# Pooled values of batch 0 summed in PSUM from the tokens' rows, wider filler matmuls, and new numbers for the planner

## The chip, the cores and the metric

The kernel runs on one NeuronCore of a Trainium2 chip. The metric is device time in microseconds (us) for one execution of the program. TensorE (PE), VectorE (DVE), ScalarE (ACT), GpSimd (POOL) and SyncE (SP) each take their instructions in a fixed order and wait for one another by semaphores; SP issues nearly all DMAs.

## The reference, cut to what matters

q, k, v are (4, 8, 576, 64), all float32. `x` has 2304 rows of 512.

```python
q_d, k_d, v_d = (t.reshape(B, H, 144, 4, D).mean(axis=3) for t in (q, k, v))
out_d = softmax(q_d @ k_d.T / 8) @ v_d                # pooled attention, 144 x 144
out_local = softmax(where(|i - j| < 4, q @ k.T / 8, -1e9)) @ v
x = (repeat(out_d, 4, axis=2) + out_local)            # to 2304 x 512
h = x @ moe_w_in;   x = elu(h) @ moe_w_out            # 512 -> 2048 -> 512
h = x @ moe2_w_in;  return (s * relu(h)**2 + b) @ moe2_w_out
```

## The kernel before, in words

**Feed-forward layers.** Every operand is split into a high part that TensorE multiplies at its fast float32 rate and a low part, the rest; a product is three passes (high x high, low x high, high x low). Phase 0 is the first layer, phase 1 the second. Tokens go in groups j of 256 (or 512 where "wide"), the 2048 hidden columns in 16 blocks f. `ffn_h` (matmuls at L894) makes the hidden block, ScalarE, VectorE and GpSimd apply the activation and split it, `ffn_x` (L960 to L967) multiplies it on into PSUM. The weights of phase 0 pass once through two staging buffers `raw`: two DMAs of 512 KB (L347, L351), then a chain on ScalarE (L356), VectorE (L359, L364), ScalarE (L303, the high part) and GpSimd or VectorE (L311, the low parts, 512 columns each) into `w0` to `w15`. In phase 0 the groups j = 0 and j = 1 run interleaved, j = 1 behind j = 0 by `LB` blocks, so that each weight block serves both while the others are still on their way.

**Attention.** Batches 0 and 1 work in units of two heads (`hp` = 0 to 3), batches 2 and 3 in another way. Batch 0 comes first of all, since nothing else can run without it; its data lie in the not yet used weight buffers: q and k in `w4` to `w7`, v in `w8` to `w11`, transposed q and k, pooled sums and the pooled v (`vd`) in `w12` to `w15`. `attention0` does the first half (288 tokens) of each unit, `attention0_rest` the second. The steps of a half: `tr` transposes (L535) and pools by a reduce (L541); `gs` makes pooled scores (L562) and their softmax; `ls` makes local scores (L647, L654) and their softmax; `gpt_` and `lpt_` transpose the probabilities (L610, L711); `gpv` multiplies the pooled ones by `vd` (L627); `lpv` multiplies the local ones by windows of v (L726), adds `up`, the result of `gpv`, and splits the sum into the operand x of phase 0.

**The pooled values.** `vg` holds, per partition, the four tokens of one pooled position side by side, for four head halves. `vsum` adds them in two tensor_tensor instructions (L548: 512 columns, in place; L549: 256 columns into `vd`), on GpSimd or VectorE. The late windows of v (`loads_late`, the second half's, L485) land where `vg` lay and so wait for `vsum`.

**The local softmax** has two forms: with `by_act` six ScalarE exponentials with row sums per half (L681); otherwise VectorE subtracts the maximum (L688, L689) and one ScalarE exponential does all (L693), and VectorE makes the sums. In batch 0, `by_act` holds for every unit.

**The order of the work** is written out by a planner (`Plan.emit`): every operation has a cost in us per engine, a due time, buffers and dependencies. It steps through a modelled time, picks per engine the operation that is ready and due first (with rules `HOLD`, `GROUP`, `WAIT`), and emits it. A DMA's length in the model is its bytes at 255 GB/s, times `slow`. Due times come from anchors (`T0`, `P0`, `TR`, `A1`, ...), pulled earlier by what depends on them. Where PE is idle in the model, `keep_warm` fills the time with matmuls on zeros (L1178, 128 columns each), so that its clock stays up.

**The end.** The last group's outputs leave through `ev` and `xr` buffers; the last two accumulators are copied in halves, by ScalarE and VectorE, and SP issues the DMAs (L989).

Of the kernel before, what the change touches and what calls it, by code (L numbers as in the profile page):

```python
# [22 lines left out]
EARLY = 1  # L23
ACT_EXP = 2
NLP = 2

T0, P0, LB, TR, R0, P1, P2 = 36.7, 5.112, 5, 34.78, 2.153, 2.551, 2.603
VO, N0, N1, WL, RL, A1, A2, A3, AE, XL = 1.82, -8.98, 62.49, 12.66, -44.23, 25.59, -36.48, 2.6, 63.87, 29.58  # L30
DE, DS, DT = -11.16, 96.84, 75.88
LASTP, NREST, VP = 2, 5, -9.3
# [22 lines left out]
class Plan:  # L55
# [5 lines left out]
    SLACK = 0.0  # L61
    GROUP = 18.61
    SWITCH = 0
    HOLD = 0.057
    WAIT = 1.615
# [162 lines left out]
def attn_moe_moe2(ctx, tc, q, k, v, w_in, w_out, w2_in, w2_out, s2, b2, mask, mask_d, out):  # L228
# [105 lines left out]
    def weights(ph, f):  # L334
# [9 lines left out]
        for i in range(2):  # L344
            def ld(i=i):
                if i == 0:
                    nc.sync.dma_start(  # L347
                        out=raw()[:, 0].rearrange("p (c f) w -> p c (f w)", c=CC),
                        in_=wi[:, f * 128:(f + 1) * 128].bitcast(I32).rearrange("(c p) f -> p c f", p=128))
                else:  # L350
                    nc.sync.dma_start(  # L351
                        out=raw()[:, 1].rearrange("p f w -> p (f w)"), in_=wo[f * 128:(f + 1) * 128, :].bitcast(I32))

            load(rawp[i], 524288, ld, due - RL, u=[raw])

# [41 lines left out]
    class Unit:  # L397
# [46 lines left out]
        def loads(self, due, late=0, nb=0.0, nb_late=0.0):  # L444
# [9 lines left out]
            def parts(i, n0, n1, late):  # L454
                for a in range(2):
                    e = "act" if a and not late and b == 0 and hp < 2 else "sp"
                    load(self.natp[i, n0 // NQB], 24576 * (n1 - n0),
                         lambda a=a, e=e: nat(i, n0, n1, a, nc.scalar if e == "act" else nc.sync),
                         due + (late if late else 0), u=[self.nat], slow=1.2, nb=nb + (nb_late if late else 0), queue=e)

# [11 lines left out]

            load(self.vg, 294912, vg, due + VO, u=self.both if b == 0 else (), nb=nb)

# [13 lines left out]
            def loads_v(half):  # L488
                for a in range(2):
                    load(self.vwp[half], VR * NQB * CT * 256, lambda a=a: vw(half, a),  # L490
                         due + VO + (late if half else 0), r=[self.vd] if b == 0 and half else (), u=self.both,
                         n=3 if (b, hp, a, half) == (0, 0, 0, 0) else 1, slow=1.2, nb=nb + (nb_late if half else 0))

# [51 lines left out]
        def vsum(self, due):  # L545
            def f(e):
# [4 lines left out]
            op(("pool", "dve"), (2.1, 1.3), (lambda: f(nc.gpsimd), lambda: f(nc.vector)),  # L551
               r=[self.vg], w=[self.vg, self.vd], u=self.both + self.tdv if self.b == 0 else (), due=due, lock=True)

# [65 lines left out]
        def gpv(self, halves, due):  # L619
            n = len(halves)  # L620
            ps = self.ps([128, n * G], "h" if halves[0] == 0 else "at")
            pt = [self.gpt[a, halves] for a in range(2)]

            def pe():
                for a in range(2):
                    for kc in range(2):
                        nc.tensor.matmul(ps()[a * D:(a + 1) * D, :], lhsT=self.vd()[:, 2 * a + kc, :],  # L627
                                         rhs=pt[a][0]()[:, pt[a][1], kc, :], start=(kc == 0), stop=(kc == 1))

            op("pe", 0.1 + 0.24 * n, pe, r=[self.vd, pt[0][0], pt[1][0]], w=[ps], u=self.tdv, due=due)  # L630
            if self.b >= DIRECT:
# [30 lines left out]
        def softmax(self, pss, half, due):  # L662
# [55 lines left out]
        def lpv(self, half, due):  # L718
# [19 lines left out]
            for j in range(2) if b == 0 else ():  # L738
                lo, hi = max(j * N, t0), min((j + 1) * N, t0 + HS)
                if hi > lo:  # L740
                    split(x_buf(0, j), hp, lo - j * N, hi - lo, lambda lo=lo, hi=hi: xf(lo - t0, hi - lo), [x], due)
            lo = max(t0, 2 * N) if b == 0 else t0
# [138 lines left out]
    def ffn_h(ph, j, f):  # L881
# [18 lines left out]
        if (ph, j) == (0, 0) and f < EARLY:  # L900
            runs = [([(0, 0, c), (1, 0, c), (0, 1, c)], [w_hi, w_lo, *x.part[c]]) for c in range(CC)]
        elif f == 0 or (ph, j) == (0, 0):
# [40 lines left out]
    def ffn_x(ph, j, f, g):  # L943
# [8 lines left out]
        for k, a in enumerate((2, 3, 0, 1) if two and last else range(tiles)):  # L952
# [19 lines left out]
            final = ph == 1 and j == NSUB - 2  # L972
            o = Buf(p2, "xr" if final and k < 2 else "ev", [128, 512])
            if ph == 0:
# [7 lines left out]
                continue  # L982
            parts = 2 if final and k >= 2 else 1
            n = 512 // parts
            for i in range(parts):
                half, c = Buf(None, "half", None), slice(i * n, (i + 1) * n)
                copy(lambda o=o, c=c: o()[:, c], lambda acc=acc, c=c: acc()[:, c], n, ("act", "dve")[i:] if parts > 1 else ("act", "dve"),
                     r=[acc], w=[half], u=[o], due=due - 4)
                load(Buf(None, "out", None), 262144 // parts, lambda a=a, o=o, c=c: nc.sync.dma_start(  # L989
                    out=out[j * N + a * 128:j * N + (a + 1) * 128, c], in_=o()[:, c]), due, r=[half], u=[o])  # L990

# [45 lines left out]
    def attention0():  # L1037
# [28 lines left out]
    def attention0_rest():  # L1066
        second = (1,)

        def A(u, d):
            u.tr(1, 1, d)  # L1070

# [102 lines left out]
    def keep_warm(slot, us, cold):  # L1174
        pool, tag = slot
        o = pool.tile([128, 128], F32, tag=tag, name=tag)
# [66 lines left out]
```

## Time and profile before

| | us |
|---|---|
| time, median of 3 runs (lowest, highest) | 951.03 (948.11, 952.88) |
| profiled execution, its own time | 953.3 |
| its span, first to last instruction | 951.5 |
| PE busy | 939.4 (99%) |
| DVE, ACT, POOL busy | 522.2, 438.9, 414.0 |
| mean granted TensorE clock | 0.995 |

The page's second part divides the span into 40 slices of 23.8 us; a digit is the busy share in tenths. Matmuls are pipelined, their ends are modelled, and fillers count as busy, so a 9 for PE doesn't say that it did useful work.

```profile
PE   8899999999999999999999999999999999999998
DVE  5466768887998969887245864222222322222221
ACT  6587775555544555444656664222322232223222
POOL 4477566798887786875556744000200110000000
PEclk9799999999999999999999999999999999999999
DMA  9739676543434543333244461000200010001001
```

### The profile page before, as it was taken

To read this page: it belongs to the slowest core of one execution; us is meant where nothing else is said; L and a number is where in the kernel's file an instruction comes from. 1 tells how busy PE (TensorE), PEld (TensorE's weight loads), DVE (VectorE), ACT (ScalarE), POOL (GpSimd) and SP (SyncE) were. 2 spreads that over 40 slices of the span, in tenths; PEclk is the share of its full clock that TensorE was granted. 3 is DMA by queue.
4 is the path that set the end of the run, shared out by engine and by line. 5 is a ranking of instruction groups with operands and counts; after the bars stand their busy time and mean duration, and the time that the engine had idled before them with its cause. 6 is when DMAs were issued, how large, how long until landed. Compare 5 with 4: busy or idle time off the path is not lost.

```text
span 951.5 us, 18034 instructions
## 1 busy us (share of the span) xinstructions
PE 939.4 (99%) x7096; PEld 826.2 (87%) x7096; DVE 522.2 (55%) x868; ACT 438.9 (46%) x1068; POOL 414.0 (44%) x378
## 2 busy tenths in 40 slices
PE   8899999999999999999999999999999999999998
PEld 7888999999999999999888898888888888888886
DVE  5466768887998969887245864222222322222221
ACT  6587775555544555444656664222322232223222
POOL 4477566798887786875556744000200110000000
PEclk9799999999999999999999999999999999999999
DMA  9739676543434543333244461000200010001001
GB/s 193 213 106 218 194 197 156 141 132 100 121 93 107 125 114 100 75 105 117 82 162 147 159 226 45 23 1 0 67 23 1 13 54 1 1 1 45 0 1 45
DMA packets 101941, 88.14 MB, mean 93 GB/s; under 512 B 48864, under 2 KB 90848, under 8 KB 101856
## 3 DMA queue, kind: packets, MB, share of 16 engines
q1 hardware_dynamic: 100064, 86.54, 32.4%
q8 instruction: 56, 0.92, 0.4%
q10 hardware_dynamic: 1792, 0.44, 0.2%
q14 instruction: 29, 0.24, 0.1%
HBM read 73.85 MB, written 13.11 MB: 91 GB/s over the span
## 4 chain that ended last, share of the span: by engine, by line
PE 88%; DVE 4%; ACT 2%; issue 2%; DMA 2%; POOL 2%; SPq 0%; DVEq 0%; POOLq 0%; ACTq 0%
PE h L894 37%; PE acc L964 14%; PE acc L967 12%; PE at L967 9%; PE acc L894 2%; PE at L960 2%; PE acc L960 2%; PE at L726 1%; PE at L1178 1%; DMA nat<-in_q_dram 1%; DVE raw L834 1%; DMA vg<-in_v_dram 1%; PE acc L1178 1%; PE at L627 1%; PE h L726 1%
## 5 line engine op out<-in xcount | busy, mean ns | idle before, releaser
L894 PE MATMUL h<-x,w 128*128 128x256 f32 (+1 forms) x1936 | 342.4, 323 | 1.4 <-DVE r L927 0.6
L894 PEld LDWEIGHTS h<-x,w 128*128 128x128 f32 x1936 | 285.1, 189 | 34.5 <-DVE r L927 1.3
L964 PE MATMUL acc<-gh,w 128*128 128x256 f32 x896 | 147.7, 286 | 0.0
L964 PEld LDWEIGHTS acc<-gh,w 128*128 128x128 f32 x896 | 122.3, 189 | 2.6 <-issue 1.9
L933 DVE SCALAR_TENSOR_TENSOR wu<-wu,sb,h 128x512 f32<-128x512 f32 x64 | 47.8, 747 | 128.5 <-ACT wu L932 128.5
L311 POOL TENSOR_TENSOR gl<-r,gh 128x256 fp32r<-128x256 f32 x98 | 88.9, 911 | 44.7 <-ACT gh L303 40.5
L932 ACT ACTIVATE wu<-h 128x512 f32<-128x512 f32 x64 | 38.3, 598 | 127.2 <-PE h L894 126.8
L311 POOL TENSOR_TENSOR w<-raw,w 128x512 fp32r<-128x512 f32 x50 | 68.7, 1390 | 50.3 <-ACT w L303 49.6
L964 PE MATMUL acc<-gl,w 128*128 128x256 f32 x448 | 89.9, 282 | 0.0
L964 PEld LDWEIGHTS acc<-gl,w 128*128 128x128 f32 x448 | 68.8, 188 | 0.0
L303 ACT ACTIVATE gh<-r 128x256 fp32r<-128x256 f32 x109 | 44.4, 413 | 44.1 <-PE acc L964 22.3
L834 DVE TENSOR_REDUCE raw<-wu 128x128 f32<-128x896 f32 x36 | 63.5, 1791 | 1.6 <-POOL wu L311 1.6
L311 POOL TENSOR_TENSOR wu<-raw 128x896 f32<-128x896 f32 x28 | 59.8, 2147 | 9.1 <-DVE raw L834 7.8
L923 ACT ACTIVATE r<-h 128x256 f32<-128x256 f32 x92 | 34.8, 378 | 59.8 <-PE h L894 32.1
L927 DVE SCALAR_TENSOR_TENSOR r<-r,h 128x256 f32<-128x256 f32 x92 | 37.6, 414 | 33.5 <-ACT r L925 31.4
L311 POOL TENSOR_TENSOR nat<-xr,x 128x256 fp32r<-128x256 f32 (+1 forms) x16 | 17.1, 1085 | 86.5 <-PE h L894 77.9
L894 PE MATMUL h<-nat,w 128*128 128x512 f32 x192 | 52.4, 394 | 0.0
L364 DVE SCALAR_TENSOR_TENSOR raw<-raw 128x1024 int32<-128x1024 int32 x32 | 46.7, 1460 | 9.3 <-ACT raw L356 8.0
L311 POOL TENSOR_TENSOR raw<-xr,x 128x256 fp32r<-128x256 f32 x16 | 12.1, 783 | 88.5 <-DVE x L305 80.6
L925 ACT ACTIVATE r<-r 128x256 f32<-128x256 f32 x112 | 46.7, 417 | 2.8
L894 PEld LDWEIGHTS h<-nat,w 128*128 128x128 f32 x192 | 36.0, 188 | 8.5
L303 ACT ACTIVATE w<-raw 128x1024 fp32r<-128x1024 f32 x32 | 36.4, 1138 | 10.7 <-DVE raw L364 10.4
(188 smaller groups left out, 1649.1 us busy)
## 6 DMA issues: line engine op xcount, KB each, us to landing
raw<-in_moe_w_in_dram SPq DMA_DIRECT2D x32, 512.0 KB
raw<-in_moe_w_out_dram SPq DMA_DIRECT2D x32, 512.0 KB
raw<-in_k_dram SPq DMA_DIRECT2D x17, 320.0 KB
raw<-in_v_dram SPq DMA_DIRECT2D x17, 320.0 KB
x2d<-ev SPq DMA_DIRECT2D x18, 256.0 KB
xr<-x2d SPq DMA_DIRECT2D x18, 256.0 KB
out_dram<-ev SPq DMA_DIRECT2D x14, 256.0 KB
vg<-in_v_dram SPq DMA_DIRECT2D x12, 288.0 KB
```

Of the source, the lines that this page charges most:

```text
L303: a = (0.11 + n / 1200, lambda: nc.scalar.activation(out=out(), in_=src(), func=ACTF.Copy, scale=scale))
L311: f = lambda e: lambda: e.tensor_tensor(out=out(), in0=in0(), in1=in1(), op=alu)
L364: nc.vector.scalar_tensor_tensor(out=low(), in0=high(), scalar=3, in1=low(), op0=ALU.logical_shift_left, op1=ALU.bitwise_or)
L834: op("dve", 0.07 + 14 * D / 546, lambda: nc.vector.tensor_reduce(out=vo()[:, WD + j * D:WD + (j + 2) * D].rearrange("p (j d) -> p j d", j= ...
L894: nc.tensor.matmul(ps(), lhsT=w()[:, wpart, 0, c * 128:(c + 1) * 128], rhs=x.at(xpart)[:, c, :], start=first and i == 0, stop=last and i = ...
L925: op("act", ta, lambda: nc.scalar.activation(out=e(), in_=e(), func=ACTF.Exp, scale=-1.0), r=[r1], w=[r2], u=[e], due=due)
L927: op("dve", td, lambda: nc.vector.scalar_tensor_tensor(out=e(), in0=e(), scalar=-1.0, in1=ps(), op0=ALU.add, op1=ALU.max), r=[r2, ps], w=[ ...
L932: op("act", ta, lambda: nc.scalar.activation(out=e(), in_=ps(), func=ACTF.Relu), r=[ps], w=[r1], u=[e], due=due)
L933: op("dve", td + 0.07, lambda: nc.vector.scalar_tensor_tensor(out=e(), in0=e(), scalar=sb2[:, 0:1], in1=ps(), op0=ALU.mult, op1=ALU.mult), ...
L960: nc.tensor.matmul(acc(), lhsT=wo[:, a * 128:(a + 1) * 128], rhs=g(), start=first, stop=end)
L964: nc.tensor.matmul(acc()[:, c * N:(c + 1) * N], lhsT=wo[:, cc * 128:(cc + 1) * 128], rhs=g(), start=first and c == 0, stop=end and c == 1)
L967: nc.tensor.matmul(acc(), lhsT=g()[:, a * 128:(a + 1) * 128], rhs=wo, start=first, stop=end)
```

## The change

- `gpv` for the first halves of batch 0 multiplies the probabilities by the four rows of `vg` directly: 8 matmuls per head that add up in PSUM, not 2 on `vd`; the two heads alternate. It no longer needs `vsum`, and is costed 1.3 us.
- `vsum` of batch 0 moves from `attention0` to `attention0_rest`, and waits for that `gpv` (`g1`), as it writes `vg` in place; the late windows of v follow it.
- The local softmax of unit hp = 3 of batch 0 leaves the `by_act` form (`ACT_EXP`, and `hp % 2` becomes `hp`).
- Fillers are 512 columns wide (the zero tile read four times by a broadcast), with 128-column ones for the rest.
- DMA lengths in the planner's model: weights 0.72 (1.0 before), `vg` 0.8 (1.0), q, k and windows of v 1.38 (1.2). `HOLD` goes to 0, `GROUP` to 18.85.
- Anchors: `T0` 38.32, `P0` 4.508, `LB` 4, `TR` 24.02, `P1` 2.468, `VO` 2.88, `RL` -33.19, `DE`, `DS`, `DT` slightly; the pieces of x of a first half that belong to group j = 1 are due 10 us later (`X1`).
- The first `ffn_h` has its last contraction block in two runs, the low part of x alone in the second.
- At the end the halves have buffers of their own, VectorE copies the first and ScalarE the second, whose DMA ScalarE issues.

```diff
-ACT_EXP = 2
+ACT_EXP = 3
-T0, P0, LB, TR, R0, P1, P2 = 36.7, 5.112, 5, 34.78, 2.153, 2.551, 2.603
+T0, P0, LB, TR, R0, P1, P2 = 38.32, 4.508, 4, 24.02, 2.153, 2.468, 2.603
+X1 = 10.0
-    HOLD = 0.057
+    HOLD = 0
...
-               r=[self.vg], w=[self.vg, self.vd], ...
+               r=[self.vg] + ([self.g1] if self.b == 0 else []), w=[self.vg, self.vd], ...
...
+            raw = self.b == 0 and halves[0] == 0
+            parts = [(kc, r) for kc in range(2) for r in range(4 if raw else 1)]
             def pe():
-                for a in range(2):
-                    for kc in range(2):
-                        nc.tensor.matmul(ps()[a * D:(a + 1) * D, :], lhsT=self.vd()[:, 2 * a + kc, :],
-                                         rhs=pt[a][0]()[:, pt[a][1], kc, :], start=(kc == 0), stop=(kc == 1))
+                for kc, r in parts:
+                    for a in range(2):
+                        w = self.vg()[:, 2 * a + kc, r * D:(r + 1) * D] if raw else self.vd()[:, 2 * a + kc, :]
+                        nc.tensor.matmul(ps()[a * D:(a + 1) * D, :], lhsT=w, rhs=pt[a][0]()[:, pt[a][1], kc, :],
+                                         start=(kc, r) == parts[0], stop=(kc, r) == parts[-1])
-            by_act = self.b == 0 and self.hp % 2 < ACT_EXP
+            by_act = self.b == 0 and self.hp < ACT_EXP
...
-            u.gs((0, 1), first, d), u.ls(0, d), u.vsum(d + VP)
-            u.loads_late()
+            u.gs((0, 1), first, d), u.ls(0, d)
...
-            u.tr(1, 1, d)
+            u.vsum(d + VP), u.loads_late(), u.tr(1, 1, d)
...
-        for _ in range(int(us / (128 / (1200.0 if cold else 2400.0) + 0.003))):
-            nc.tensor.matmul(o, lhsT=wz, rhs=wz, start=True, stop=True)
+        for n in (512, 128):
+            one = n / (1200.0 if cold else 2400.0) + 0.004
+            for _ in range(int(us / one)):
+                nc.tensor.matmul(o[:, :n], lhsT=wz, rhs=wz[:, None, :].to_broadcast([128, n // 128, 128]), start=True, stop=True)
+                us -= one
```

## Rows read from the trace of the kernel before

**Rows 1.** Busy time by stage: us, each engine's busy (instructions), clock, DMA, GB/s

```profile
0.00:38.00 38.00, 32.61 (x582) 28.67 (x583) 19.73 (x58) 24.60 (x104) 18.69 (x37) 0.94 0.95 199
38.00:90.00 52.00, 50.97 (x724) 46.37 (x725) 29.86 (x71) 38.37 (x132) 33.39 (x33) 0.95 0.64 170
90.00:300.00 210.00, 208.40 (x2262) 198.65 (x2262) 171.87 (x309) 120.15 (x336) 160.23 (x144) 1.00 0.52 140
```

**Rows 2.** The same stages, line L1178 alone: PE, PEld busy

```profile
0.00:38.00 38.00, 13.34 (x167) 12.08 (x167) 0.94 0.95 199
38.00:90.00 52.00, 11.15 (x139) 8.58 (x139) 0.95 0.64 170
```

**Rows 3.** Chain of work that ended last, 0 to 60 us: start, us, what

```profile
18.51 0.41 PE h L627 x8
...
19.15 0.46 PE acc L654 x34
19.61 1.17 PE h L726 x36
20.78 0.65 PE at L535 x6
...
28.49 2.36 issue
...
32.47 1.52 PE h L726 x36
33.99 0.68 PE h L627 x8
34.68 1.16 PE at L535 x6
35.83 2.06 PE h L726 x36
37.90 1.58 PE h L894 x6
...
49.93 0.80 PE at L1178 x14
```

**Rows 4.** DMA queues, 28 to 31 us: kind, packets, MB, share

```profile
q8 instruction: 1, 0.02, 2.8%
```

**Rows 5.** Busy time by stage, 33.2 to 43.5 us (columns as in Rows 1)

```profile
33.20:43.50 10.30, 10.30 (x102) 9.52 (x99) 4.70 (x7) 5.23 (x12) 5.87 (x6) 0.50 0.56 152
```

**Rows 6.** Line L681 by stage: ACT busy (instructions), clock, DMA, GB/s

```profile
22.00:28.00 6.00, 1.72 (x12) 1.00 1.06 342
```

**Rows 7.** Lines L688, L689, L693: durations min/median/max in ns

```profile
L688 DVE TENSOR_REDUCE lmx<-at x16: 253/265/276, 91.3 to 185.9; 96x3 f32<-96x114 f32 x16
L689 DVE TENSOR_TENSOR p<-at,lmx x16: 272/273/274, 91.6 to 186.2; 96x114 f32<-96x114 f32 x16
L693 ACT ACTIVATE p<-p x8: 382/396/416, 92.4 to 186.5; 96x228 f32<-96x228 f32 x8
```

**Rows 8.** POOL in order of time: start, us, line, idle before and its end

```profile
22.00 1.26 POOL L548 TENSOR_TENSOR w<-w 72x512 f32<-72x512 f32 x1 [0.23 <-DMA w<-in_v_dram]
23.35 0.82 POOL L549 TENSOR_TENSOR w<-w 72x256 f32<-72x256 f32 x1
...
34.05 1.30 POOL L311 TENSOR_TENSOR w<-raw,w 128x512 fp32r<-128x512 f32 x1 [4.73 <-ACT w L303]
```

**Rows 9.** SP in order of time: start, us, line

```profile
32.26 3.13 SPq L485 DMA_DIRECT2D w<-in_v_dram  x4
...
39.16 0.38 SPq L347 DMA_DIRECT2D raw<-in_moe_w_in_dram  x1
```

**Rows 10.** ACT in order of time: start, us, line

```profile
46.97 1.14 ACT L356 ACTIVATE raw<-raw 128x1024 f32<-128x1024 f32 x1
```

**Rows 11.** Chain of work that ended last, 938 to 952 us

```profile
947.46 0.39 ACT ev L303
...
947.88 0.42 DVE ev L305
```

More of the change, by code (lines that the diff above doesn't have):

```diff
@@ L61 @@
     SLACK = 0.0
-    GROUP = 18.61
+    GROUP = 18.85
     SWITCH = 0
-    HOLD = 0.057
+    HOLD = 0
     WAIT = 1.615
@@ L352, in ld @@
                         out=raw()[:, 1].rearrange("p f w -> p (f w)"), in_=wo[f * 128:(f + 1) * 128, :].bitcast(I32))
-            load(rawp[i], 524288, ld, due - RL, u=[raw])
+            load(rawp[i], 524288, ld, due - RL, u=[raw], slow=0.72)
         op("act", 0.11 + 2 * DM / 1200, lambda: nc.scalar.activation(
@@ L458, in parts @@
                          lambda a=a, e=e: nat(i, n0, n1, a, nc.scalar if e == "act" else nc.sync),
-                         due + (late if late else 0), u=[self.nat], slow=1.2, nb=nb + (nb_late if late else 0), queue=e)
+                         due + (late if late else 0), u=[self.nat], slow=1.38, nb=nb + (nb_late if late else 0), queue=e)
             parts(0, 0, 2 * NQB, 0)
@@ L471, in vg @@
                     in_=v[b, 2 * hp:2 * hp + 2].rearrange("a (h i r) d -> i (a h) (r d)", h=2, r=4))
-            load(self.vg, 294912, vg, due + VO, u=self.both if b == 0 else (), nb=nb)
+            load(self.vg, 294912, vg, due + VO, u=self.both if b == 0 else (), nb=nb, slow=0.8)
             def vw(half, a):
@@ L491, in loads_v @@
                          due + VO + (late if half else 0), r=[self.vd] if b == 0 and half else (), u=self.both,
-                         n=3 if (b, hp, a, half) == (0, 0, 0, 0) else 1, slow=1.2, nb=nb + (nb_late if half else 0))
+                         n=3 if (b, hp, a, half) == (0, 0, 0, 0) else 1, slow=1.38, nb=nb + (nb_late if half else 0))
             loads_v(0)
@@ L551, in vsum @@
             op(("pool", "dve"), (2.1, 1.3), (lambda: f(nc.gpsimd), lambda: f(nc.vector)),
-               r=[self.vg], w=[self.vg, self.vd], u=self.both + self.tdv if self.b == 0 else (), due=due, lock=True)
+               r=[self.vg] + ([self.g1] if self.b == 0 else []), w=[self.vg, self.vd], u=self.both + self.tdv if self.b == 0 else (), due=due, lock=True)
         def gs(self, heads, halves, due):
@@ L740, in lpv @@
                 if hi > lo:
-                    split(x_buf(0, j), hp, lo - j * N, hi - lo, lambda lo=lo, hi=hi: xf(lo - t0, hi - lo), [x], due)
+                    split(x_buf(0, j), hp, lo - j * N, hi - lo, lambda lo=lo, hi=hi: xf(lo - t0, hi - lo), [x], due + (X1 if j > half else 0))
             lo = max(t0, 2 * N) if b == 0 else t0
@@ L900, in ffn_h @@
         if (ph, j) == (0, 0) and f < EARLY:
-            runs = [([(0, 0, c), (1, 0, c), (0, 1, c)], [w_hi, w_lo, *x.part[c]]) for c in range(CC)]
+            runs = [([(0, 0, c), (1, 0, c), (0, 1, c)], [w_hi, w_lo, *x.part[c]]) for c in range(CC - 1)]
+            runs += [([(0, 0, CC - 1), (1, 0, CC - 1)], [w_hi, w_lo, x_hi[-1]]), ([(0, 1, CC - 1)], [w_hi, x_lo[-1]])]
         elif f == 0 or (ph, j) == (0, 0):
@@ L972, in ffn_x @@
             final = ph == 1 and j == NSUB - 2
-            o = Buf(p2, "xr" if final and k < 2 else "ev", [128, 512])
+            parts = 2 if final and k >= 2 else 1
+            os = [Buf(p2, "xr" if final and (k < 2 or i) else "ev", [128, 512]) for i in range(parts)]
+            o = os[0]
             if ph == 0:
@@ L982, in ffn_x @@
                 continue
-            parts = 2 if final and k >= 2 else 1
             n = 512 // parts
[L985 to L990, printed above, removed]
+            for i, o in enumerate(os):
+                c = slice(i * n, (i + 1) * n)
+                copy(lambda o=o, n=n: o()[:, :n], lambda acc=acc, c=c: acc()[:, c], n, ("act", "dve")[1 - i:][:1] if parts > 1 else ("act", "dve"),
+                     r=[acc], w=[o], due=due - 4)
+                e = "act" if parts > 1 and i else "sp"
+                load(Buf(None, "out", None), 262144 // parts, lambda a=a, o=o, c=c, n=n, e=e: (nc.scalar if e == "act" else nc.sync).dma_start(
+                    out=out[j * N + a * 128:j * N + (a + 1) * 128, c], in_=o()[:, :n]), due, r=[o], queue=e)
     def load_x(ph, j):
```

10 lines of the change are left out of this document (6 added, 4 removed).

## The prediction

> **What bounds the kernel now.** I read the page's busy shares first, then the stages, then the chain of waits and the queues of the first 90 us. PE is busy 99% of the span, so at first sight only less matmul work could help. The stages say otherwise. From 90 us on PE is busy 208.4 of 210 us [rows 1], and nearly all of that is real work: that part moves as a block. The first 90 us are not so full: 167 of the 582 matmuls before 38 us, and 139 of 724 up to 90 us, are fillers [rows 1, 2]. A stretch of 14 fillers takes 0.80 us in the chain [rows 3], 57 ns each; that makes 167 x 57 ns = 9.5 us and 139 x 57 ns = 7.9 us in which PE had nothing to do. Before 38 us other engines and the DMA queues (share 0.95) make the operand x; between 38 and 90 us PE waits for weight blocks and for the second halves. So the end is set by how soon the first 90 us come to full work, and what they save the rest keeps.
>
> Two losses stand out in the chain. At 28.49 PE stands still for 2.36 us for nothing that the profile shows ("issue"), in the middle of a stretch of fillers, where no semaphore can hold it [rows 3]. In those 3 us one 16 KB packet of PE's instruction queue was moved (q8), with the DMA queues full [rows 4]: I read it as PE running out of instructions. After it the clock falls: 0.50 from 33.2 to 43.5 us, the lower of its two levels, 1.2 GHz [rows 5].
>
> **The change part by part.** The sum is made against the profiled execution: span 951.5 us, own time 953.3 us. The median of the runs is 951.03, 2.27 less; I take that off at the end.
>
> *The instruction wait and the clock.* A wide filler does the work of four narrow ones, so 167 become 42 or somewhat more, say 65: about 100 matmuls, each with its weight load, leave PE's instruction stream before 38 us. The pooled sums put back 24 per unit (below), 72 for three units before the wait: the stream up to 28 us is a little shorter, and filler time no longer uses it up at one matmul per 57 ns. The late windows of v, two DMAs for each of four units, the last of them issued at 32.3 to 35.4 us now [rows 9], move behind vsum and leave the crowded queue. Both ends are open: the wait may stay (0) or go (-2.36). I take -2.36, the nearer since filler speed is what emptied the buffer. If PE doesn't stand still, the clock has no reason to fall there; what it cost before the first ffn_h is read from the same instructions at both levels: L726 1.52 and 2.06 against 1.17, L627 0.68 against 0.41, L535 1.16 against 0.65 [rows 3], together 0.35 + 0.89 + 0.27 + 0.51 = 2.02 us. Ends 0 and -2.02; I take -2.02. The lower clock after 38 us I cost at nothing: fillers lie between the ffn_h there and would take the room. A wide filler itself isn't in the trace; it fills planned idle time, so at four times 57 ns it costs 0, and an overrun by one filler, 0.23 us, in each of some ten stretches bounds it at +2.3. What gives way: 0.
>
> On the first of these the Trainium skill (Runtime: NRT & Kernel Launch, Instruction fetch mechanics) says that instructions are refilled in blocks of 16 KiB, 256 instructions, and that crossing a block is mostly hidden. The block's size is the q8 packet's; the hiding is not what the 2.36 us show. By that rule a shorter instruction stream brings nothing, and the sum is 4.4 us smaller; that is case C below.
>
> *The pooled sums on PE.* gpv of a first half now takes 8 matmul instructions in 0.41 us, 51 ns each [rows 3]; four rows instead of one make it 32, 1.64 us, +1.23. Its rate among alternating heads isn't shown: the nearest rows are L654's 34 in 0.46 us, 14 ns each, which would make 32 of them 0.43 (+0.02), and L627 at the lower clock, 0.68/8 = 85 ns, 2.72 (+2.3). I take 51 ns, the same instruction. For units 0 to 2 it lies in filler time (9.5 us before 38 us, of which it takes 3.7; were that cover gone it would cost those 3.7); for unit 3 it is in the chain between the transposed probabilities and the first ffn_h: +1.23.
>
> The skill (TensorE: Matmul & The Clock Gate, Part 3) says that matmuls whose outputs lie in different column groups of the array run at the same time. L726, which alternates the heads so, takes 1.17/36 = 33 ns against 51 [rows 3], and agrees in sign; at 33 ns the term would be +0.65, not +1.23.
>
> *vsum off the way.* It takes 1.26 + 0.82 = 2.08 us per unit on POOL [rows 8], 8.3 in all, ahead of the softmax products at 9 to 24 us. Unit 3's path comes last and doesn't pass it, so I take 0 (ends 0 and -2.08). In its new place POOL has gaps (4.73 us idle before 34.05 [rows 8]; 33.4 of 52 us busy from 38 to 90 [rows 1]), so again 0; without that cover see case D. It now waits for gpv, and POOL is in order: behind it wait the low parts of weights and x, and on SP the late windows of v, and behind those the weight loads.
>
> *Unit 3's softmax.* Its exponentials take 1.72 us of ACT with 12 instructions [rows 6]. The other form needs one of 0.40, and two subtractions of 0.27 on DVE; the maxima are taken in both [rows 7]: -1.72 + 0.40 + 0.54 = -0.78. ACT is where unit 3 waits then, so I count all of it (ends 0 and -0.78; the longer row sums could take 0.3 of it).
>
> *First ffn_h, then.* -2.36 - 2.02 + 1.23 - 0.78 = -3.93 us. The split of its last block and the later due time of the j = 1 pieces take DVE and POOL work off that place; 0, ends -0.7 and 0.
>
> *38 to 90 us.* The weights decide: block 2's load goes out at 39.16, when a staging buffer is free, and its ScalarE step runs at 46.97 [rows 9, 10]; the 7.8 us between them are transfer. The buffer is freed by the same DVE and POOL queues that the start holds up, so the 3.93 us are passed on. What is late next: POOL and ACT, which have the second halves and weights at once. `TR` makes the second halves due 10.8 us earlier and `LB` = 4 brings j = 1 in one block sooner, which gives PE work where it had fillers. Ends 0 and -7.9; I take a third, -2.6, since the stage stays bound by blocks that come one by one. The other anchors act where PE is full: 0.
>
> *The end.* The last two copies run one behind the other, ScalarE at 947.46 and VectorE at 947.88 for 0.42 us [rows 11]; side by side that is -0.42.
>
> Sum: -3.93 - 2.6 - 0.42 = -6.95; 953.3 - 6.95 = 946.35, and less the 2.27 of the profiled execution 944.1 us.
>
> **The rivals.**
>
> A, the forecast: 944.1, by itself 940.5 to 948.
>
> B, the fillers between 38 and 90 us nearly all go (-7.9 instead of -2.6): 938.8. For it: the fillers lie there because PE has no work ready, and `TR` and `LB` are both about that. Against: POOL and ACT are busy for 33.4 and 38.4 of 52 us [rows 1], and a block passes four steps on them.
>
> C, the instruction wait only moves: the boundary is met a little later with the queues still full, PE stands still as long, and the clock falls. Then 2.36 + 2.02 stay: 948.5. For it: 72 of the 100 matmuls saved come back as pooled sums, and the weights' loads stay in the queue. Against: the late windows leave it. The page's rule ends at the same time by another reason.
>
> D, slower: vsum in its new place holds up the weights. It sits in POOL's queue behind gpv and ahead of low parts; a late window on SP waits for it, and the load of block 2 behind that. Three units' sums (the first has the idle 4.73 us) make 3 x 2.08 = 6.24 us. The start's gain isn't seen then, as blocks decide from 39 us on: 951.03 + 6.24 - 0.42 = 956.9. It decides from the point where vsum of unit 3 ends later than 39.16, when the staging buffer is free anyway [rows 9]. For it: gpv of unit 3 runs at 34 us [rows 3], so 36 at best. Against: there are 3 us between.
>
> **How the numbers follow.** A 0.43, B 0.13, C 0.22, D 0.22. A measurement of this kernel tells 0.5% from no change, 4.76 us: faster is under 946.3, slower over 955.8. Faster: 0.33 of A, B's 0.13, 0.02 of C: 0.48. Same: 0.10 of A, 0.18 of C, 0.03 of D: 0.31. Slower: 0.19 of D, 0.02 of C: 0.21. The range 938 to 956 leaves out some 0.04 of B and 0.12 of D.
>
> **What would show it.** Right: no idle time of PE of over 1 us within fillers before 35 us; granted clock 1.0 up to 50 us; first ffn_h near 34 us, not 37.9 [rows 3]; L627 of a first half 32 instructions in about 1.6 us; L356 of the third block near 43 us; fewer than 90 narrow fillers' worth of L1178 time (5 us) between 38 and 90 us. Wrong: a wait of POOL's L548 for PE with L311 of weights behind it, an SP issue of L485 that stands before L347 beyond 40 us, or a first ffn_h at 37 us or later.

## The result

| | before | changed |
|---|---|---|
| median, us (lowest, highest; 4 runs each) | 949.76 (948.11, 952.88) | 960.51 (959.46, 961.75) |
| profiled execution: own time, span | 953.3, 951.5 | 961.75, 960.0 |
| mean granted clock | 0.995 | 0.988 |

The changed kernel is slower: ratio 1.0105, 95% interval 1.0086 to 1.0124. The forecast, 944.1, had the wrong sign, and the time lies above the range. The medians are 10.75 us apart, the two spans read below only 8.4: the profiled execution of before is 3.5 us above this median, that of the changed kernel 1.2 above its own.

### The profile after

The stages of the changed kernel, columns as in [rows 1], all work first, then the fillers (L1188 now) alone, as in [rows 2]:

```profile
0.00:38.00 38.00, 33.58 (x549) 24.06 (x550) 20.02 (x63) 21.79 (x89) 17.84 (x35) 0.93 0.90 188
38.00:90.00 52.00, 48.19 (x578) 36.17 (x578) 29.06 (x66) 32.44 (x100) 31.96 (x30) 0.89 0.61 174
90.00:300.00 210.00, 208.71 (x2235) 198.27 (x2232) 173.92 (x313) 124.85 (x349) 159.57 (x142) 0.99 0.51 139
```
```profile
0.00:38.00 38.00, 11.65 (x49) 5.17 (x49) 0.93 0.90 188
38.00:90.00 52.00, 16.52 (x66) 6.05 (x66) 0.89 0.61 174
```

From 38 to 90 us PE is busy 2.8 us less than in [rows 1], and 16.52 us of it are fillers instead of 11.15 [rows 2]: 8.2 us less useful work, part of it at the lower clock (0.89 against 0.95). The stage from 90 us on is as full as before.

How long the first part lasts is read from line L900 (L894 before), the `ffn_h`. Each group j issues 192 of its matmuls in phase 0, so the 385th begins j = 2, which needs x of batch 1 and comes behind j = 0 and j = 1. Before, in 0 to 195.2 and from there on (PE, PEld busy):

```profile
0.00:195.20 195.20, 58.06 (x384) 50.36 (x385) 0.97 0.68 173
```

The changed kernel:

```profile
0.00:206.10 206.10, 57.25 (x385) 50.23 (x385) 0.95 0.64 170
```

j = 2 begins at 206.1 us instead of 195.2, 10.9 later. From there to PE's last matmul 749.0 us pass instead of 752.2 (3.2 are given back), and from that matmul to the end of the span 4.88 instead of 4.10. Together 10.9 - 3.2 + 0.8 = 8.5 us, the difference of the spans.

The start, PE's instructions in order of time (start, busy us, line, tile, form, idle before and what ended it), where [rows 3] had the wait of 2.36 us and the first `ffn_h` at 37.90:

```profile
28.77 1.22 PE L631 MATMUL h<-pt,w 72*64 72x72 f32 x32
29.92 1.00 PE L732 MATMUL h<-pt,w 38*64 38x32 f32 x27
31.53 0.47 PE L732 MATMUL h<-pt,w 38*64 38x32 f32 x9 [0.61 <-issue]
31.93 1.60 PE L631 MATMUL h<-pt,w 72*64 72x72 f32 x32
...
36.66 2.13 PE L732 MATMUL h<-pt,w 38*64 38x32 f32 x36
38.72 3.60 PE L1188 MATMUL acc<-wz 128*128 128x512 bf16 x8
41.76 1.46 PE L900 MATMUL h<-x,w 128*128 128x256 f32 x5
```

The wait has shrunk to 0.61 us, and still the clock is low, in the stretch of [rows 5]:

```profile
33.20:43.50 10.30, 9.32 (x71) 6.60 (x68) 4.93 (x9) 5.40 (x11) 8.24 (x8) 0.53 0.53 144
```

so that eight wide fillers take 3.60 us, 0.45 each, and the first `ffn_h` stands behind them at 41.76. Meanwhile POOL has the moved `vsum` of two units ahead of the low parts of x and of a weight:

```profile
32.05 1.26 POOL L549 TENSOR_TENSOR w<-w 72x512 f32<-72x512 f32 x1
33.39 1.23 POOL L550 TENSOR_TENSOR w<-w 72x256 f32<-72x256 f32 x1
34.58 1.27 POOL L549 TENSOR_TENSOR w<-w 72x512 f32<-72x512 f32 x1
35.92 0.73 POOL L550 TENSOR_TENSOR w<-w 72x256 f32<-72x256 f32 x1
37.55 0.72 POOL L312 TENSOR_TENSOR x<-xs,x 128x256 fp32r<-128x256 f32 x1 [0.90 <-ACT x L304]
38.24 1.29 POOL L312 TENSOR_TENSOR w<-raw,w 128x512 fp32r<-128x512 f32 x1
```

The second loss lies at 70 to 92 us. Blocks 2 to 4 of j = 0 begin at 53.3, 58.5 and 66.3 us, within 2 us of before (51.4, 57.1, 66.6), though 3 to 5 us behind e15, an execution of the old order shown below; block 5 begins at 92.1 instead of 72.9. The second halves of batch 0 are multiplied at 65.2, 73.3, 83.3 and 89.0 us, before at 59.1, 65.4, 71.7 and 78.2. The chain of the changed kernel there:

```profile
83.43 0.16 DVE grs L594
...
83.87 0.27 DVE p L695
...
84.78 0.46 DVE xs L738
...
85.94 2.04 POOL p L312
...
88.02 0.48 PE at L717 x3
...
88.99 1.24 PE at L732 x36
...
92.36 3.69 PE h L900 x24
```

The last second half of batch 0 is multiplied at 88.99 us, and only then run 24 `ffn_h` in a piece. Among them are those of weight block 5 for j = 0, whose low parts POOL had done by 77.7 us:

```profile
75.09 2.61 POOL L312 TENSOR_TENSOR w<-raw,w 128x512 fp32r<-128x512 f32 x2 [1.18 <-ACT w L304]
```

With `LB` = 4 the first block of j = 1 is written ahead of block 5 of j = 0. It needs the second half of every unit, PE takes its instructions in order, and so a block that could run at 78 us waits to 92. Before, with `LB` = 5, block 5 ran at 72.86.

The tail, where [rows 11] had the two copies one behind the other:

```profile
954.42 0.42 DVE L306 COPY ev<-acc 128x256 f32<-128x256 f32 x1 [6.19 <-PE acc L974]
...
955.84 0.38 ACT L304 ACTIVATE xr<-acc 128x256 f32<-128x256 f32 x1 [1.46 <-DMA out_dram<-xr]
956.25 0.38 ACTq L998 DMA_DIRECT2D out_dram<-xr  x1
956.73 0.38 ACT L304 ACTIVATE xr<-acc 128x256 f32<-128x256 f32 x1 [0.51 <-DMA out_dram<-xr]
```

ScalarE's halves go into `xr`, which earlier output DMAs still read: it waits 1.46 and 0.51 us for them, more than the copy of 0.42 that was to be saved.

### The profile page after: what moved, and what is told of

Same layout as the page of the kernel before. It is cut to its first block, busy times and chain, and to the rows that moved or that the text cites. A ratio compares the mean times of both kernels' runs of the same rounds, so it can differ in the third digit from the quotient of the medians.

```text
span 960.0 us, 17700 instructions
## 1 busy us (share of the span) xinstructions
PE 945.3 (98%) x6931; PEld 818.3 (85%) x6931; DVE 519.3 (54%) x869; ACT 439.0 (46%) x1045; POOL 424.3 (44%) x382
## 4 chain that ended last, share of the span: by engine, by line
PE 89%; DVE 4%; DMA 3%; ACT 2%; POOL 1%; issue 1%; SPq 1%; ACTq 0%; DVEq 0%; POOLq 0%
PE h L900 39%; PE acc L971 15%; PE acc L974 12%; PE at L974 9%; PE acc L900 3%; PE at L967 2%; PE acc L967 2%; PE at L732 1%; DMA w<-in_v_dram 1%; DMA raw<-in_moe_w_out_dram 1%; PE acc L1188 1%; PE at L631 1%; DVE raw L365 1%; PE at L563 1%; PE at L611 1%
## 5 line engine op out<-in xcount | busy, mean ns | idle before, releaser
L900 PE MATMUL h<-x,w 128*128 128x256 f32 (+1 forms) x1936 | 340.8, 322 | 0.4 <-DVE r L934 0.2
L900 PEld LDWEIGHTS h<-x,w 128*128 128x128 f32 x1936 | 284.8, 189 | 33.0 <-issue 1.0
L312 POOL TENSOR_TENSOR gl<-r,gh 128x256 fp32r<-128x256 f32 x103 | 86.8, 846 | 42.5 <-ACT gh L304 39.6
L312 POOL TENSOR_TENSOR w<-raw,w 128x512 fp32r<-128x512 f32 x53 | 73.7, 1408 | 37.0 <-ACT w L304 36.4
L312 POOL TENSOR_TENSOR wu<-raw 128x896 f32<-128x896 f32 x30 | 65.5, 2194 | 11.4 <-DVE raw L840 10.8
L934 DVE SCALAR_TENSOR_TENSOR r<-r,h 128x256 f32<-128x256 f32 x92 | 37.8, 413 | 35.6 <-ACT r L932 32.7
L900 PE MATMUL h<-nat,w 128*128 128x512 f32 x192 | 52.4, 394 | 0.0
L900 PEld LDWEIGHTS h<-nat,w 128*128 128x128 f32 x192 | 36.0, 187 | 8.5
```

Of the source, the lines that this page charges most:

```text
L312: f = lambda e: lambda: e.tensor_tensor(out=out(), in0=in0(), in1=in1(), op=alu)
L900: nc.tensor.matmul(ps(), lhsT=w()[:, wpart, 0, c * 128:(c + 1) * 128], rhs=x.at(xpart)[:, c, :], start=first and i == 0, stop=last and i = ...
L934: op("dve", td, lambda: nc.vector.scalar_tensor_tensor(out=e(), in0=e(), scalar=-1.0, in1=ps(), op0=ALU.add, op1=ALU.max), r=[r2, ps], w=[ ...
```

## Experiments

Ratios are to the kernel before in the same comparison, with 95% intervals; by the same measure the changed kernel stands at 1.0105. Starts in us are read as above: the first `ffn_h`; the last group of 36 `lpv` matmuls of batch 0's second halves and of batch 1; the 385th `ffn_h`. Ratios come from all runs, starts from one profiled execution each. The row "before" is the execution with the standstill of 2.36 us; e15, whose compute engines do the same work in the same order up to the last copies, shows this kernel without it.

| | ratio | first ffn_h | batch 0, last | batch 1, last | j = 2 | span |
|---|---|---|---|---|---|---|
| before | 1 | 37.8 | 78.2 | 191.8 | 195.2 | 951.5 |
| changed | 1.0105 | 41.8 | 89.0 | 201.7 | 206.1 | 960.0 |
| e1 changed, LB 5 | 1.0242 | 38.7 | 84.0 | 205.1 | 211.4 | 969.2 |
| e2 before, LB 4 | 1.0127 | 35.4 | 74.8 | 197.7 | 202.7 | 961.2 |
| e3 changed, one row | 1.0112 | 42.5 | 87.8 | 201.9 | 206.3 | 960.3 |
| e4 changed, narrow fillers | 1.0115 | 39.0 | 85.5 | 198.2 | 202.6 | 957.8 |
| e5 before, raw sums | 1.0091 | 38.5 | 81.1 | 200.2 | 202.0 | 957.9 |
| e6 changed, no raw sums | 1.0161 | 38.5 | 82.0 | 204.9 | 209.1 | 966.0 |
| e7 before, new lengths | 1.0153 | 36.0 | 85.7 | 207.7 | 211.1 | 965.7 |
| e8 before, new anchors | 1.0260 | 41.7 | 80.6 | 203.1 | 209.3 | 977.0 |
| e9 before, wide fillers | 0.9996 | 35.1 | 76.6 | 189.6 | 192.9 | 949.1 |
| e10 changed, half vsum | 1.0108 | 41.5 | 87.6 | 201.6 | 206.0 | 959.9 |
| e11 e2, light scores | 1.0134 | 35.4 | 74.2 | 200.0 | 205.0 | 959.9 |
| e12 changed, light scores | 1.0106 | 42.6 | 88.8 | 201.6 | 206.0 | 959.2 |
| e13 changed, no fillers from 36 us | 1.0090 | 39.8 | 84.6 | 198.7 | 203.1 | 956.8 |
| e14 changed, old anchors | 1.0172 | 40.2 | 90.7 | 207.3 | 209.0 | 964.7 |
| e15 before, new end | one run | 35.6 | 74.7 | 188.4 | 191.8 | 949.6 |
| e16 before, wide fillers, own end | 0.9982 | 34.7 | 74.4 | 187.4 | 190.6 | 946.8 |

**e1, e2: the order of the blocks.**

```diff
-T0, P0, LB, ... = 38.32, 4.508, 4, ...
+T0, P0, LB, ... = 38.32, 4.508, 5, ...      (e1; e2 is the reverse, 5 to 4, in the kernel before)
```

> The changed kernel with LB = 5 instead of 4, all else kept. Theory B (block order): in the changed kernel the first ffn_h of group j = 1 stands ahead of block 5 of j = 0 in PE's order and waits for unit 3's second half until 92 us, while block 5's weights are there at 77.7. With LB = 5 block 5 runs before it. Of the 9 us of useful matmul work by which the changed kernel is behind at 100 us, 8 arise between 70 and 100 us; theory B gets most of it back: 953 to 956, and ffn_h work of block 5 starts before 82 us. Theory R (the sums by rows on PE, and their GpSimd sums behind them, delay the start, and all later steps with it): 959 to 962, and the second halves' L732 stay after 65 us.

> The kernel before with LB = 4 instead of 5, all else kept. Theory B: block 5 falls behind the first ffn_h of j = 1, which has its operand at 84.9 us, and PE loses what it did for block 5 from 73 us on: 953 to 957. Theory R: LB does not matter much: 949 to 952.

e1 973.93, ratio 1.0242 (1.0205 to 1.0280); e2 963.29, 1.0127 (1.0107 to 1.0146). Both are slower than either theory allowed. In e1 block 5 does run early, at 70.8 us, and yet the time is longer: the loss has moved. Fillers of e1 by stage (PE, PEld busy):

```profile
38.00:90.00 52.00, 14.43 (x62) 5.25 (x60) 0.98 0.62 182
90.00:180.00 90.00, 0.56 (x4) 0.27 (x4) 1.00 0.57 163
180.00:220.00 40.00, 16.57 (x83) 7.41 (x83) 1.00 0.56 149
```

Before has 3.46 us of them in 180 to 220. PE is through with j = 0 and j = 1 and stands, while batch 1's last units go through the engines one by one: j = 2 needs both. e2 shows the same from the other side, with 12.25 us of fillers there. So two chains must meet at j = 2: PE's own work, and batch 1's attention. In the changed kernel it is the first that comes late. Its fillers from 90 us to j = 2, and those of e2:

```profile
90.00:206.00 116.00, 1.17 (x5) 0.47 (x5) 0.99 0.57 162
```
```profile
90.00:202.60 112.60, 11.83 (x191) 10.77 (x192) 1.00 0.59 162
```

`LB` = 5 makes the changed kernel slower and `LB` = 4 the kernel before: which one is right depends on the other numbers.

**e3, e10: the raw sums and vsum by themselves.** e3 leaves out three of the four rows, so that `gpv` has 8 matmuls again; e10 leaves out the first addition of batch 0's `vsum`. The order is the changed kernel's.

```diff
-                for kc, r in parts:
+                done = [p for p in parts if p[1] == 0]
+                for kc, r in done:
```
```diff
-                e.tensor_tensor(out=vg[:, :, 0:2 * D], in0=vg[:, :, 0:2 * D], in1=vg[:, :, 2 * D:4 * D], op=ALU.add)
+                if self.b:
+                    e.tensor_tensor(out=vg[:, :, 0:2 * D], in0=vg[:, :, 0:2 * D], in1=vg[:, :, 2 * D:4 * D], op=ALU.add)
```

> The changed kernel, whose first-half gpv multiplies one of the four token rows alone (the other three are left out of the sum); the planner's costs and so the order on every engine stay. PE has 24 matmul instructions fewer per unit, 0.8 to 1.2 us each unit, two of them (units 2 and 3) one behind the other ahead of the first ffn_h. Theory R: the start comes 2 to 3 us earlier and all of it is kept, 956.5 to 958.5. Theory B: PE waits for unit 3's second half anyway, but that half starts earlier as well; 1 to 2 us, 958.5 to 959.5.

> The changed kernel whose vsum of batch 0 leaves out the first of its two additions (its pooled values of the second half are then those of two tokens of four): 1.26 us of GpSimd less per unit, same order on every engine. Rival D of the prediction (vsum on GpSimd holds up the weights): the second halves' L732 come 2 to 5 us earlier, 955 to 958. Otherwise: 959 to 961.5.

e3 961.98, 1.0112 (1.0092 to 1.0132); e10 961.27, 1.0108 (1.0083 to 1.0133): both the changed kernel's time, though both theories expected e3 to be 1 to 4 us faster. In e3 PE waits 2.0 and 1.9 us for ScalarE's transposed probabilities `pt` ahead of the first `ffn_h`, which comes at 42.5 us: what PE saves there it waits. Neither PE's time in the raw sums nor the 1.26 us of POOL's in `vsum` is what costs.

**e4, e9, e13: the fillers.** e4 gives the changed kernel narrow fillers, e9 the kernel before wide ones, e13 leaves out what the planner puts in after its 36 us.

```diff
-            if idle > 0.2:
+            if idle > 0.2 and t0 < 36.0:        (e13)
```

> The changed kernel with the fillers of before, 128 columns each; the order on every engine stays, since the planner does not count fillers. Theory W (wide fillers hold the clock worse and overrun): the clock does not fall at 73 and 90 us and falls for less long at 33; 954 to 957. Theories B and R: 959 to 962, slower rather than faster by up to 2 us where PE's instruction stream gets short again (idle of over 1 us with no releaser before 40 us).

> The kernel before with the wide fillers alone; the order on every engine stays. As the prediction had it (fewer instructions, no instruction wait, no lower clock, and the start's gain kept): no idle time of PE over 1 us before 35 us, first ffn_h at 34 to 35 instead of 37.8 us, 945 to 948. Theory W (wide fillers hold the clock worse): first ffn_h at 38 to 42, 951 to 955. Theory S (j = 2 waits for batch 1, whatever the start does): 949 to 951 even with the earlier start.

> The changed kernel without the fillers that the planner puts in after its 36 us (the real work and its order stay). Theory, that fillers only fill time in which PE has nothing to do: first ffn_h and the second halves of the units (89.0 us for the last) move by under 2 us, j = 2 begins at 204 to 208, and the time stays at 958 to 963 us; if the clock falls for longer without fillers, it may be up to 968. Rival, that fillers at half the clock hold PE up in 38 to 92 us: the 6.6 us of fillers on the chain go, the last second half comes at 82 to 84 us, j = 2 at 199 to 201, and the time is 953 to 956 us.

e4 959.84, 1.0115 (1.0049 to 1.0181); e9 950.86, 0.9996 (0.9980 to 1.0011); e13 959.37, 1.0090 (1.0066 to 1.0115). In their profiled executions e4 and e13 bring the first `ffn_h` 2.8 and 2.0 us sooner, and j = 2 by 3.5 and 3.0, in e13 between what the theory and its rival expected; the median times are within 1.2 us of the changed kernel's, inside the intervals (e4's is some 12 us wide). So wide fillers hold back little that the runs can tell. Without fillers the clock from 38 to 90 us is 0.80 instead of 0.89, lowest at its end; e13:

```profile
70.00:80.00 10.00, 8.64 (x112) 7.30 (x113) 6.97 (x16) 6.75 (x25) 7.11 (x7) 0.71 1.05 230
80.00:90.00 10.00, 8.36 (x71) 7.07 (x72) 5.25 (x10) 3.95 (x9) 3.30 (x3) 0.50 0.39 127
```

e9 tests the prediction's first steps: the old order, no standstill of PE over 1.0 us, granted clock 1.00 in each 5 us from 20 to 45, first `ffn_h` at 35.1. What was forecast of wide fillers came, and the time is the same. But 35.1 is early only beside the one profiled execution of before. e2, e11 and e15 have narrow fillers and the order of before on the four compute engines up to 67.9 us, and their first `ffn_h` comes at 35.4, 35.4 and 35.6: beside these, wide fillers bring 0.3 to 0.5 us. In this order they do hold the clock; 35 to 40 us in before, e2, e15 and e9:

```profile
35.00:40.00 5.00, 5.00 (x55) 4.62 (x54) 3.95 (x7) 3.04 (x9) 3.25 (x5) 0.50 0.29 55
```
```profile
35.00:40.00 5.00, 5.00 (x35) 4.75 (x34) 2.33 (x5) 1.58 (x3) 3.50 (x5) 0.50 0.46 90
```
```profile
35.00:40.00 5.00, 5.00 (x50) 4.75 (x47) 2.99 (x5) 2.40 (x6) 4.62 (x5) 0.66 0.46 101
```
```profile
35.00:40.00 5.00, 4.38 (x32) 3.17 (x29) 3.07 (x6) 2.70 (x7) 4.45 (x5) 1.00 0.33 67
```

**e5 to e8, e14: the parts one by one.** e5 has the raw sums and the moved `vsum` in the kernel before, e6 the changed kernel without them; e7 the new DMA lengths alone, e8 the new anchors alone; e14 the changed kernel with the old anchors.

```diff
-            load(rawp[i], 524288, ld, due - RL, u=[raw])
+            load(rawp[i], 524288, ld, due - RL, u=[raw], slow=0.72)      (e7, and the others likewise)
```
```diff
-T0, P0, LB, TR, R0, P1, P2 = 36.7, 5.112, 5, 34.78, 2.153, 2.551, 2.603
+T0, P0, LB, TR, R0, P1, P2 = 38.32, 4.508, 4, 24.02, 2.153, 2.468, 2.603      (e8, with the other anchors; e14 the reverse)
```

> The kernel before with the sums by rows alone: gpv of the first halves on the four rows of vg, vsum of batch 0 behind it in attention0_rest, the late windows of v behind that; numbers, lengths, fillers and softmax form as before. Theory R (the sums by rows and the later vsum cost the 9 us): 957 to 962. Theory O (the new numbers give an order of work that fits the chip worse; the sums by rows are harmless): 949 to 954. Theory S (in all kernels the end is the first ffn_h of group j = 2 plus 754 to 759 us of span, and that ffn_h comes a few us after the last L726 of batch 1): holds in either case.

> The changed kernel with the sums by rows undone: vsum ahead of gpv and in attention0, as before; all else of the change kept. Theory R: 949 to 953. Theory O: 957 to 965, since the numbers stay. Theory S: span minus the start of the first ffn_h of j = 2 is 754 to 759 us.

> The kernel before with the new DMA lengths in the planner's model alone (weights 0.72, vg 0.8, q, k and v windows 1.38). Theory O, if the lengths are what misfits: 955 to 965; if it is the anchors: 948 to 953. Theory S as above.

> The kernel before with the new anchors alone (T0, P0, LB, TR, P1, VO, RL, DE, DS, DT, X1, GROUP, HOLD); lengths, sums, fillers and softmax form as before. Theory O, if the anchors are what misfits: 957 to 965, with the last L726 of batch 1 after 198 us; if it is the lengths, or the sums: 948 to 953. Theory S as above.

> The changed kernel with the anchors, HOLD, GROUP and LB of before; the lengths, the raw sums, the fillers and the end stay changed. Theory, that the numbers are fitted jointly, so that old anchors don't suit the new lengths: slower than the changed kernel, 963 to 975 us. Rival, that the new anchors (LB = 4 above all) are by themselves what makes the changed kernel slow: block 5 of j = 0 no longer waits for unit 3, and the time is 950 to 956 us.

e5 959.94, 1.0091 (1.0061 to 1.0120); e6 967.19, 1.0161 (1.0116 to 1.0206); e7 966.22, 1.0153 (1.0115 to 1.0191); e8 977.44, 1.0260 (1.0220 to 1.0301); e14 967.87, 1.0172 (1.0150 to 1.0194). Each of these parts alone is slower than before, the new anchors most, and taking one out of the changed kernel makes that slower still. e6, e7 and e8 are slower than either theory allowed. The new softmax form, the later due time `X1` and the split of the first `ffn_h` were not tried alone. The changes don't add up: 0.9% for e5, 1.5% for e7 and 2.6% for e8, and 1.05% for all together. Lengths, `gpv`'s cost and anchors are inputs of one planner that writes out the whole order, and the runs agree with numbers that were fitted jointly: half of them changed is worse than none or all. (e5 also changes what `vsum` and the late windows of v wait for, so it is not an input alone.) What they do to the order shows in the table: in e5, e7 and e8 the second halves of batch 0 end 2.4 to 7.5 us late, and batch 1 8.4 to 15.9, each some 3.4 more beside e15's row. Theory S of the expectations holds: from the start of j = 2 to the end of the span it takes 753.1 to 758.5 us in every profile but e8's (767.8).

**e11, e12: competition for VectorE and GpSimd.** In both, the scores of the directly computed rows of attention are taken over 8 of 64 dimensions (56 are left out), which takes work off both engines in the same written order; e11 on e2, e12 on the changed kernel.

```diff
-            tt(lambda: x()..., lambda: pair(kq, j, [[D, 2], [D, 7], [1, D]]), ...
+            tt(lambda: x()[:, :, :, :8], lambda: pair(kq, j, [[D, 2], [D, 7], [1, 8]]), ...
```

> The kernel before with LB = 4, in which the scores of batches 2 and 3's direct rows use 8 of 64 dimensions (the rest is left out): their products on GpSimd and sums on VectorE shrink to an eighth, the order stays. With LB = 4 alone PE is 1.8 us ahead of the kernel before at 125 us, then runs fillers from 180 to 215 us while batch 1 is unfinished: 963.3. Theory S: batch 1 shares VectorE and GpSimd with these rows and now ends earlier: last L726 of batch 1 before 193 (197.7 with LB = 4 alone), first ffn_h of j = 2 before 198 (202.7), 952 to 958. If PE's own work sets j = 2: 961 to 964.

> The changed kernel with the same light scores. Its PE has 0.7 us of fillers between 130 and 205 us. If its end is set by PE's own backlog from the first 100 us: 958 to 961. If batch 1's chain alone sets it: 950 to 955.

e11 963.43, 1.0134 (1.0096 to 1.0172), no faster than e2: it isn't the load on these engines that holds up batch 1's last units. e12 960.69, 1.0106 (1.0081 to 1.0131): that load isn't the cause in the changed kernel either, as expected if PE's own backlog sets j = 2.

**e15, e16: the end.** e15 has the changed end alone. e16 has wide fillers and an end whose second halves go into buffers that no DMA reads:

```diff
-            os = [Buf(p2, "xr" if final and (k < 2 or i) else "ev", [128, 512]) for i in range(parts)]
+            os = [Buf(p2, "wu" if i else "xr" if final and k < 2 else "ev", [128, 512]) for i in range(parts)]
```

> The kernel before with the changed end alone. The order up to the end is that of before. Theory (from the tail of the changed profile): ScalarE's last two copies wait for output DMAs that still read their buffer, 0.5 to 1.5 us each, and from the last matmul to the end of the span it takes 4.7 to 5.1 us, against 4.1 before; time 951.5 to 952.5. The prediction's own step: 0.42 us less, 3.7 us from the last matmul to the end.

> The kernel before with wide fillers and with an end whose second halves have buffers that no DMA reads (the activation's, free by then). Theory: nothing holds the copies up, from the last matmul to the end 3.6 to 4.0 us, and the start is that of the kernel before with wide fillers (first ffn_h at 35.1, j = 2 at 192.9); time 947.5 to 950.5 us, 0.997 to 1.000 of before, perhaps not to be told from it. Rival, that what the start and the end save is lost in between: 951 to 953 us.

e15 951.37, one run. Its last matmul ends at 944.72 and its span at 949.60: 4.88 us, as in the changed kernel, against 4.10 before. In all ten profiles with the changed end it is 4.87 to 4.90, in the seven with the old one 4.10 to 4.12. The step that was to bring 0.42 costs 0.78. e16 949.64 (12 runs) against 950.99 (17 runs): ratio 0.9982 (0.9968 to 0.9996), the only interval that lies below 1, and barely; 3.97 us from the last matmul to the end, of which 0.13 is saved, so that the end explains little of the 1.35. Its ScalarE copies no longer wait for a DMA:

```profile
942.22 0.38 ACT L303 ACTIVATE wu<-acc 128x256 f32<-128x256 f32 x1
942.64 0.38 ACTq L991 DMA_DIRECT2D out_dram<-wu  x1
```

e15 also says something that it wasn't made for. Up to the end its 7096 matmul records are those of the kernel before, one by one in the same order, fillers included. Here is where [rows 3] had the standstill:

```profile
26.17 1.24 PE L726 MATMUL h<-pt,w 38*64 38x32 f32 x36
...
27.64 2.68 PE L1180 MATMUL at<-wz 128*128 128x128 bf16 x45
...
35.62 1.65 PE L894 MATMUL h<-x,w 128*128 128x256 f32 x6
```

and its stretch of [rows 5]:

```profile
33.20:43.50 10.30, 10.27 (x128) 9.72 (x127) 5.15 (x9) 6.43 (x16) 6.87 (x7) 0.83 0.71 209
```

45 fillers in 2.68 us without a gap, clock 0.83 instead of 0.50, the first `ffn_h` at 35.6, and j = 2 at 191.8 instead of 195.2. e2 and e11 do stop, at the same filler as before, the 41st, but not as long:

```profile
29.45 0.45 PE L1178 MATMUL at<-wz 128*128 128x128 bf16 x5 [0.84 <-issue]
```
```profile
30.25 0.45 PE L1178 MATMUL at<-wz 128*128 128x128 bf16 x5 [0.56 <-issue]
```

The last packet of q8 ahead of that filler ended at 29.52 us in before, at 27.72 in e2 and at 28.85 in e11, and PE went on 1.3, 1.7 and 1.4 us after it. In e15 it ended at 27.90, and PE reached the filler 2.0 us later, without a gap. That agrees with the prediction's reading, that PE ran out of instructions, and with a wait that is as long as the block is late; that it was this block which held the filler is not shown. So the place belongs to the kernel, and the 2.36 us, the longest of four executions, do not; the lower clock behind it comes with a short wait or none, too.

## Why the prediction was wrong

**The failed step is "38 to 90 us", with "the other anchors act where PE is full: 0".** It was put at -2.6 us, a third of 7.9 us of fillers filled, on top of the start's 3.93 passed on. Measured: 8.2 us less useful work in that stage, and j = 2 begins 10.9 us later. `LB` = 4 was to give PE work where it had fillers; the fillers grew from 11.15 to 16.52 us. `TR` was to make the second halves due 10.8 us earlier; they came 6.1 to 11.6 us later. The step took the written order as given and moved it earlier; but `LB`, `TR`, the lengths and `gpv`'s cost make the planner write another order, and e2, e5, e7 and e8 show that parts of the change alone cost 0.9 to 2.6%. That price was not in the rows of the old order; it should have stood as a term of its own of some 10 us, and a rival "the new order is worse" was missing. The trace shows one concrete piece: block 5 behind j = 1's first block, ready at 77.7 and run at 92. But that isn't the whole price, as e1, which undoes it, loses more elsewhere. "The weights decide" fits up to block 4. The room was under-read, too: 139 x 57 ns makes 7.9 us, but [rows 2] have 11.15.

**The premise "what the first 90 us save the rest keeps" holds in part.** From j = 2 on it holds (753.1 to 758.5 us in every profile but one). For a loss it holds in the changed kernel as well: with 1.17 us of fillers between 90 us and j = 2, PE never makes up what it didn't do before. It fails where batch 1 comes later than PE's own work: e2 and e15 have the same order up to 67.9 us and the last second half of batch 0 at 74.8 and 74.7, but j = 2 at 202.7 and 191.8, in e2 behind 11.8 us of fillers. Full PE in [rows 1] showed that no time was lost there, not that batch 1 would keep up in another order.

**The instruction wait (-2.36) and the clock (-2.02).** Their sizes were read from one execution and taken as the kernel's. In the same order the wait is 0.84, 0.56 and 0 us in e2, e11 and e15, and the first `ffn_h` comes at 35.4 to 35.6 instead of 37.8: 2.2 to 2.4 of the 4.38 us belong to that execution, and wide fillers add 0.3 to 0.5 (e9). Beside that, the 2.27 by which that execution exceeded the median were taken off once more; as far as that excess is this wait, it was counted twice. "If PE doesn't stand still, the clock has no reason to fall there" is refuted by e15, which has 0.66 in 35 to 40 us. In the changed kernel a wait of the same kind is down to 0.61, but the low clock came back at the same place, with wide fillers: case C's clock without C's wait. What the prediction named as a sign against it, a first `ffn_h` at 37 us or later, is there (41.76). The third L356 (L357 now), forecast near 43 us, comes at 49.4. Case B's place was seen, too, but with the other sign: the fillers grew.

**The pooled sums (+1.23).** The mechanism was right and the size too large. In order of time, the 8 matmuls of before and the 8 of e3, whose heads alternate:

```profile
18.44 0.48 PE L627 MATMUL h<-pt,w 72*64 72x72 f32 x8
```
```profile
18.85 0.47 PE L632 MATMUL h<-pt,w 72*64 72x72 f32 x8
```

32 take 1.22 us: 24 more cost 0.74, 31 ns each. The 51 ns spread what a group takes once, about 0.23 us, over 8 matmuls. The 33 ns of L726 hold such a part, too (its 36 start within 1.02 us, 29 ns apart), so the comparison showed nothing of alternation. The Trainium skill (TensorE: Matmul & The Clock Gate, Part 3) says that matmuls with outputs in different column groups run at the same time; the trace doesn't bear that out here, as 8 take 0.47 us with the heads alternating and 0.48 without. e3 shows that the term isn't on the path that decides.

**vsum (0) and case D.** vsum does stand ahead of x and of weights on POOL, as D said, and a late window's issue at 40.54 us stands between two weight loads. But the load for which D named 39.16 goes out at 39.55, and the next, 44.91 instead of 41.70, at 44.63 in e10: taking 1.26 of 2.08 us per unit away changes nothing. D's place was seen, its price wasn't.

**Unit 3's softmax (-0.78).** The form changed as forecast (one exponential of 0.38, two subtractions of 0.27), but the first `ffn_h` came at 41.8 and not near 34, so nothing of it shows. In the second half the same form puts the maxima and subtractions on VectorE, where the chain runs from 83.4 to 85.8 us. This part was not tried alone.

**The end (-0.42).** +0.78, by the buffer: that "side by side" was free supposed that `xr` was. [rows 11] show the copies, not who still reads the target; the DMAs of the same buffer should have been looked up.

**Left open.** Why unit 3's second half comes 10.8 us late in the changed kernel is settled only so far: not fillers (e13: 4.4 of it at most, and not in the time), not `vsum` (e10), not the raw sums' length (e3), not VectorE's and GpSimd's load from the direct rows (e12). Nor is it the late windows of v: the last is issued at 40.54 us, the first second half is multiplied at 65.2, and from 60 to 95 us PE waits for POOL and ScalarE and for no DMA. That it is the order is argued from the parts (e5 to e8, e14); unit 3's softmax form is an untested rival, and which swap in the order costs what was not isolated.

## What to carry to other kernels

Where a planner with fitted numbers writes the order, a change of any of its inputs re-makes the whole schedule: price that as a term of its own, from what such changes cost (here 0.9 to 2.6%, always slower), before adding up what the edits do one by one. Before a loss seen in one trace becomes a term, look for its size in a second execution of the same order, and if the profiled execution is longer than the median, suspect that the loss is the difference. And an early saving counts only when every chain that meets later is followed to that meeting.

## What the runs showed of the hardware

- With one and the same PE order, four executions stood 2.36, 0.84, 0.56 and 0 us at the same filler for nothing that the profile shows; in the three that stood, PE went on 1.3 to 1.7 us after a 16 KB packet of the instruction queue q8 had ended. The granted clock in 35 to 40 us was 0.50, 0.50, 0.66 and 0.66, and with wide fillers in the same order (e9, e16) 1.00.
- A ScalarE copy into a buffer that an output DMA still reads waits that DMA out: 1.46 and 0.51 us, in the changed kernel and in e15 alike.
- 72x64 float32 matmuls on 72 columns cost 31 ns for each further one at full clock; alternating between two heads brings nothing (0.47 us for 8 in e3, 0.48 before).
- Fillers of 512 columns at the lower clock take 0.45 us each (8 in 3.60). In e13, without fillers, the granted clock was 0.50 in 80 to 90 us, where the changed kernel has 0.98, and 0.91 in 38 to 50 us, where that has 0.80.
